# A stored order for the instructions of four engines in a fused attention and MLP kernel

## The chip, the cores and the metric

The kernel runs on one core of one Trainium2 chip. The metric is device microseconds of one execution, the median of 3 runs. Five engines work in the core, each through its own queue, in order: TensorE (PE in the profile, its weight loads PEld), VectorE (DVE), ScalarE (ACT), GpSimd (POOL) and SyncE (SP, which only issues DMAs).

## The reference

Attention with 4 sink positions and a window of 128, then a two-layer MLP over all tokens, all in float32:

```python
batch, n_heads, seq, head_dim = (4, 8, 768, 64)
scores = scale * np.matmul(q, k.transpose(0, 1, 3, 2))
keep = is_sink | in_window            # pos < 4, or 0 <= i - j < 128
a = softmax(np.where(keep, scores, -1e9))
attn_out = np.matmul(a, v)
x = attn_out.transpose(0, 2, 1, 3).reshape(3072, 512)
h = x @ w_in                          # 512 x 2048
out = (h - np.tanh(h)) @ w_out        # 2048 x 512
```

## The kernel before

The 3072 tokens are cut into 12 chunks `cc` of 256 tokens. Attention of a chunk is done in 4 units `u` (a unit is a pair of heads, 48 in all), the MLP of a chunk in 8 groups `g` of 256 hidden columns, 96 steps `n` in all. The chunks' MLP steps run on PE almost without a break from about 50 us on, and the attention of later chunks is slipped in between.

The pieces of a unit, with the lines that a row shows: `scores` multiplies queries and keys on PE (L537 for the first 12 units, L544 after), `merge` masks and takes the row maximum on DVE (L559, L561), `exponent` is ACT's exponential (L569), `sums` the reciprocal on DVE (L589, L590), `scale` on ACT (L595), `sinks` on POOL (L604 to L606). `turn` then transposes the probabilities on PE into the PSUM bank `t` (L629), and three pieces copy them out of that bank into the tile `pt`: in a chunk that starts a batch `whole` on ACT (L636), and always two masked products on DVE, `below` and `after` (both L643). When 2 or 4 units are done, `attend` transposes the sink columns on PE (L670), copies them on ACT into `zr` (L677), multiplies with the values on PE (L686, L692; that reads `zr` and `pt`), and splits the result into a high and a low part on ACT (L709) and DVE (L713).

An MLP step multiplies x by a group of w_in on PE (`h`, L828), takes tanh on ACT (L859), the difference on DVE (L862), and splits it into high and low halves (L865 and L868, in the later chunks L873 to L881 for seven combined blocks); PE then multiplies these by w_out (L910, or L944 in the later chunks). The weights come as 64-bit floats: three DVE instructions decode a group's words (L157, L159, L161), ACT rounds (L752) and DVE forms the low part (L756). Later chunks read w_in's parts back from DRAM into a ring of 7 tiles, and w_out's combined blocks are formed on SP, POOL, ACT and DVE (`derive`, L1048 to L1061).

None of this is issued where it is written. Every piece is handed to `Work.add` with its engine, a duration, a due time and the names that it reads and writes, 3002 pieces in all; `Work.order` decides how they follow each other, and a loop at the end of `_banded` emits them in that order. In this version `order` is a list scheduler: it keeps a clock for each engine, and whenever an engine is free it takes, of the pieces whose inputs are done by its clocks, the one with the earliest due time. The durations, due times and waking delays are constants in the code. The order fixes the queue of each engine, and where pieces of two engines touch the same tile, which of them waits for the other.

Of the kernel before, what the change touches and what calls it, by code (L numbers as in the profile page):

```python
# [17 lines left out]
B, H, S, D = 4, 8, 768, 64  # L18
P = 128
DM = H * D  # L20
# [20 lines left out]
def kernel(  # L41
# [50 lines left out]
    with tc.If(bad == 0) as cmp:  # L92
        _banded(tc, qd, kp, vp, vs, small, masks, w_in, w_out, ident, pts, early, out)
# [76 lines left out]
class Work:  # L170

    WAKE = {"PE": 250, "ACT": 170, "DVE": 90, "POOL": 100, "SP": 80}

    def __init__(self, slack, pad, late, land):
        self.all, self.wrote, self.read = [], {}, {}
        self.slack, self.pad, self.late, self.land = slack, pad, late, land  # L180

    def add(self, engine, took, due, fn, reads=(), writes=(), lands=0, port=False):
        n = len(self.all)
# [9 lines left out]
        self.all.append((engine, took, due, fn, after - {n}, lands, port))  # L193

    def order(self):
        todo = {}
        for n, (engine, *_) in enumerate(self.all):
            todo.setdefault(engine, []).append(n)
        users, left = [[] for _ in self.all], [len(t[4]) for t in self.all]
        for n, t in enumerate(self.all):  # L200
            for a in t[4]:
                users[a].append(n)
        ready = {n: 0.0 for n, k in enumerate(left) if k == 0}
        waiting = {e: [n for n in v if n in ready] for e, v in todo.items()}
        free, port, start, done = dict.fromkeys(todo, 0.0), {}, {}, {}

        def at(n, e):
            t = max(free[e], ready[n])
            return max(t, port.get("DVE" if e == "POOL" else "POOL", 0.0)) if self.all[n][6] else t

        while any(waiting.values()):
            t, e = min((min(at(n, e) for n in v), e) for e, v in waiting.items() if v)
            n = min((n for n in waiting[e] if at(n, e) <= t), key=lambda n: (self.all[n][2], n))
            _, took, _, _, _, lands, locks = self.all[n]
            took *= self.pad if e in ("ACT", "DVE", "POOL") and self.all[n][2] > self.late else 1.0
            waiting[e].remove(n)
            start[n], free[e], done[n] = t, t + took, t + took
            if lands:
                free[e], done[n] = t + (took if e == "POOL" else lands), t + lands + (1700 if self.all[n][2] < self.late else self.land)
            if locks:  # L220
                port[e] = t + took
            for u in users[n]:
                f = self.all[u][0]
                lag = 0 if f == e else self.WAKE[e]
                if f == "PE":
                    lag += self.slack if self.all[u][2] > self.late else 100
                ready[u] = max(ready.get(u, 0.0), done[n] + lag)
                left[u] -= 1
                if not left[u]:
                    waiting[f].append(u)  # L230
        return sorted(start, key=lambda n: (start[n], n)), start


def _banded(tc, qd, kp, vp, vs, small, masks, w_in, w_out, ident, pts, early, out):
    nc = tc.nc
    et = mybir.EngineType
    with ExitStack() as ctx:
# [28 lines left out]
        RAW, TWO, CUT, DUO, SC, PB, ZL, TK = 12, 12, 2, 3, 4, 4, -4000, 1100  # L266
        SLK, PAD, LATE, LAND, QP, KP, BP, LEAD3 = 0.0, 1.05, 68932.8, 4939.1, 0, 0, 0, 92253.7
        SA, NSLOT, RING, GP, LQ, ST = 5, 7, 7, 0, 1, 1
        work = Work(SLK, PAD, LATE, LAND)

        chunks = [(b, 0) for b in range(3)] + [(b, c) for b in range(3) for c in range(1, CPB)]
        chunks += [(b, c) for b in range(3, B) for c in range(CPB)]
# [2 lines left out]
        order += [(cc, g) for g in range(CUT, NG) for cc in (2, 1)] + [(0, g) for g in range(CUT, NG)]  # L275
        order += [(cc, g) for cc in range(3, NCHUNK) for g in range(NG)]
        NS = len(order)
        FIRST, EARLY, PACE, LEAD = 45488.2, 4498.8, 8248.4, 74582.8
        UNIT, SECOND, WLEAD, WNEXT = 2182.8, 6399.4, 6045.8, 1426.5
# [6 lines left out]
        def due_unit(u):  # L286
            cc, p = divmod(u, NPAIR)
            if cc < 3:
                return UNIT * u + SECOND * cc
            return due_step(order.index((cc, 0))) - (LEAD3 if cc == 3 else LEAD) - 2 * PACE * (NPAIR - 1 - p)  # L290

        def due_group(g):
            return due_step(min(n for n, x in enumerate(order) if x[1] == g))
# [23 lines left out]
        def slot(u):  # L317

            return u % PB if u < RAW else u % 2

        def unit(u):
            cc, p = divmod(u, NPAIR)
            return (cc, p, *chunks[cc])
# [116 lines left out]
        mask, above, below, after, rest = masks  # L440
# [45 lines left out]
        qh, ql, ks, pr, st, xps, xh, xl, sps, tps = ({} for _ in range(10))  # L486
# [130 lines left out]
        def place(u):  # L617
            return u % 2 if u < DUO * NPAIR else u % NPAIR

        def turn(u):  # L620

            cc, p, b, c = unit(u)
            m = place(u)

            def transposes():
                to = tps[u] = tbank.rearrange("p (h t q) -> p h t q", h=2, t=2)
                for t in range(2):
                    for h in range(2):
                        nc.tensor.transpose(to[:, h, t, :], pr[u][:, 2 * h + t, NSK:], ident)  # L629

            w = pts[:, m].rearrange("p h (t o) q -> p (h t) o q", o=2)
            w1 = pts[:, m].rearrange("p h (t o) q -> p h t o q", o=2)

            def whole():

                nc.scalar.copy(w1[:, :, 0, 1, :], tps[u][:, :, 0, :])  # L636

            def part(o, mask):
                if c == 0:
                    src, dst, n = tps[u][:, :, 1, :], w1[:, :, 1, o, :], 2  # L640
                else:
                    src, dst, n = tps[u].rearrange("p h t q -> p (h t) q"), w[:, :, o, :], 4
                nc.vector.tensor_tensor(dst, src, mask.unsqueeze(1).to_broadcast([P, n, P]), op=ALU.mult)  # L643

            def plain():
                nc.scalar.copy(w[:, :, 0, :], tps[u].rearrange("p h t q -> p (h t) q"))

            def masked():
                nc.gpsimd.tensor_tensor(w[:, :, 0, :], w[:, :, 0, :], after.unsqueeze(1).to_broadcast([P, 4, P]), op=ALU.mult)

            d = due_unit(u) + 5500
            work.add("PE", 470, d, transposes, [("p", slot(u), 0), ("p", slot(u), 1)], ["t"])
            if c == 0:
                work.add("ACT", 260, d + 1400, whole, ["t"], [("pt whole", m)])
            work.add("DVE", 430 if c == 0 else 710, d + 1500, lambda: part(1, below), ["t"], [("pt own", m)])
            if c and BP:
                work.add("ACT", 490, d + 1500, plain, ["t"], [("pt before", m)])
                work.add("POOL", 1360, d + 1600, masked, (), [("pt before", m)], port=True)
            else:
                work.add("DVE", 430 if c == 0 else 710, d + 1500, lambda: part(0, after), ["t"], [("pt before", m)])  # L660

        def attend(cc, p0, pairs):

# [477 lines left out]
        def attention(cc):  # L1141
            if cc and chunks[cc][0] != chunks[cc - 1][0]:
                sink_values(chunks[cc][0], due_unit(NPAIR * cc) + 4000)
            for u in range(NPAIR * cc, NPAIR * cc + NPAIR):
                if not raw(u):
                    split(u)
                for t in range(2):
                    scores(u, t)
                if u == 0:
                    work.add("DVE", 400, 3000, sink_half, ["sidei", ("p", 0, 1)], ["half"])  # L1150
                    sink_values(0, 10000)
                if RAW <= u + 1 < NU:
                    load_qk(u + 1)
                normalise(u)
                turn(u)
                if cc < DUO and u % 2:
                    attend(cc, u % NPAIR - 1, 2)
            if cc >= DUO:
                attend(cc, 0, NPAIR)
            if cc + 1 < NCHUNK:  # L1160
                load_v(cc + 1)
# [11 lines left out]
        for n in range(NS):  # L1173
            cc, g = order[n]
# [5 lines left out]
            if n:  # L1180
# [3 lines left out]
                cc, g = order[n - 1]  # L1184
# [9 lines left out]
                            derive(i, m)  # L1194
        second_half(NS - 1)

        todo, _ = work.order()
        with tc.manual_schedule(engines={et.PE, et.SP, et.DVE, et.Activation, et.Pool}):
            for n in todo:
                work.all[n][3]()  # L1200
# [204 lines left out]
```

## Time and profile before

| what | value |
|---|---|
| median of 3 runs | 667.82 us (667.61 to 668.23) |
| the profiled execution's own time | 667.38 us |
| its span, first to last instruction | 665.6 us |
| PE, PEld busy | 648.9 us (97%), 603.5 us (91%) |
| DVE, ACT, POOL busy | 543.4 us (82%), 397.0 us (60%), 165.2 us (25%) |
| TensorE's mean granted clock | 0.997 of 2.4 GHz |
| DMA | 152.97 MB, mean 230 GB/s |
| last PE instruction starts | 658.21 us |

A row of the timeline gives the start and the length of an instruction, or of several equal ones that follow each other (x6). PE's instructions overlap, and the ends of its rows are modelled: a 128x256 matmul has a row of 0.28 us, while the next starts some 0.11 us after it. What PE loses is therefore read from the starts, or from the idle time named in brackets with what ended it. DVE's and ACT's rows overlap by a little too.

### The profile page before, as it was taken

Reading aid. Unit: us, or ns where it says so; the run is one execution under the profiler, and the core shown is the slowest. Engines: PE = TensorE matmul, PEld = TensorE weight load, DVE = VectorE, ACT = ScalarE, POOL = GpSimd, SP = SyncE. Lnnn points to the kernel's source line nnn. Section 1 sums busy time; section 2 is a strip of 40 time slices with the busy share of each in tenths; the row PEclk is TensorE's granted clock in tenths of the full one; section 3 lists DMA queues with packets and bytes.
Section 4 is the critical chain, followed back from the end, with each engine's and each line's share of the span. In section 5 each row is a group of like instructions: output and inputs, shape, how many; then the busy total and the mean of one; then the engine's idle time right before and its main releaser. Section 6 shows DMA issues by size and latency. Waiting matters only on the chain.

```text
span 665.6 us, 14571 instructions
## 1 busy us (share of the span) xinstructions
PE 648.9 (97%) x5111; PEld 603.5 (91%) x5111; DVE 543.4 (82%) x1399; ACT 397.0 (60%) x1024; POOL 165.2 (25%) x331
## 2 busy tenths in 40 slices
PE   7889999999999999999999999999999999999995
PEld 6668999999979889899999999999999999999995
DVE  5889999964999778578799899887899899855654
ACT  5987444345898667567665575676666566523331
POOL 5453000000873232243331212312213212100100
PEclk9999999999999999999999999999999999999998
DMA  5877788884999767899977767867776866656861
GB/s 167 290 260 283 249 277 301 289 305 128 231 204 282 219 207 227 241 265 300 301 221 221 231 199 233 252 188 212 246 222 203 263 187 204 209 166 202 262 209 37
DMA packets 79502, 152.97 MB, mean 230 GB/s; under 512 B 9596, under 2 KB 25852, under 8 KB 79420
## 3 DMA queue, kind: packets, MB, share of 16 engines
q1 hardware_dynamic: 65900, 121.52, 57.9%
q0 software_dynamic: 13376, 30.30, 16.4%
q8 instruction: 42, 0.69, 0.4%
q14 instruction: 40, 0.33, 0.1%
q10 hardware_dynamic: 144, 0.13, 0.1%
HBM read 131.47 MB, written 20.45 MB: 228 GB/s over the span
## 4 chain that ended last, share of the span: by engine, by line
PE 82%; DVE 8%; ACT 4%; issue 1%; POOL 1%; DVEq 0%; ACTq 0%; POOLq 0%
PE h L828 36%; PE s L944 11%; PE o L910 8%; PE o L944 8%; PE x L692 3%; PE s L910 3%; PE t L629 2%; PE t L692 2%; PE t L544 2%; PE x L544 2%; PE t L910 2%; PE x L910 2%; DVE pt L643 1%; PE s L544 1%; ACT p L595 1%
## 5 line engine op out<-in xcount | busy, mean ns | idle before, releaser
L828 PE MATMUL h<-xall,ring 128*128 128x256 f32 x990 | 130.1, 279 | 0.0
L828 PEld LDWEIGHTS h<-xall,ring 128*128 128x128 f32 x990 | 121.0, 188 | 1.4 <-issue 0.5
L859 ACT ACTIVATE gbuf<-h 128x512 f32<-128x512 f32 x96 | 57.2, 596 | 90.4 <-PE h L828 68.3
L828 PE MATMUL h<-xall,spare 128*128 128x256 f32 x738 | 97.4, 278 | 0.0
L878 ACT CAST ghbuf<-gbuf 128x896 fp32r<-128x896 f32 x55 | 51.7, 941 | 68.2 <-DVE gbuf L875 67.9
L828 PEld LDWEIGHTS h<-xall,spare 128*128 128x128 f32 x738 | 90.6, 188 | 0.5
L370 POOL DMA_DIRECT2D qraw<-qd x36 | 26.7, 742 | 255.4 <-DVE q L511 199.9
L881 DVE TENSOR_TENSOR glbuf<-gbuf,ghbuf 128x896 fp32r<-128x896 f32 x55 | 59.9, 1089 | 20.2 <-ACT ghbuf L878 17.3
L569 ACT ACTIVATE p<-p,st 128x132 f32<-128x132 f32 x132 | 52.4, 399 | 13.1 <-DVE st L561 12.1
L862 DVE TENSOR_TENSOR gbuf<-h,gbuf 128x512 f32<-128x512 f32 x55 | 37.9, 689 | 22.1 <-ACT gbuf L859 20.9
L910 PE MATMUL o<-w,ghbuf 128*128 128x512 f32 x192 | 49.9, 395 | 0.2 <-ACT ghbuf L865 0.2
L828 PEld LDWEIGHTS h<-xall,w 128*128 128x128 f32 x384 | 46.9, 188 | 2.1 <-DVE w L756 0.4
L828 PE MATMUL h<-xall,w 128*128 128x256 f32 x384 | 48.2, 279 | 0.2 <-DVE w L756 0.2
L502 DVE TENSOR_TENSOR ks<-kraw,ks 64x392 fp32r<-64x392 f32 x72 | 40.4, 562 | 6.0 <-ACT ks L497 3.9
L595 ACT ACTIVATE p<-p,st 128x132 f32<-128x132 f32 x132 | 42.6, 395 | 4.1 <-DVE st L590 3.5
L910 PEld LDWEIGHTS o<-w,ghbuf 128*128 128x128 f32 x192 | 33.8, 188 | 6.1 <-ACT ghbuf L865 0.5
L862 DVE TENSOR_TENSOR h<-h,gbuf 128x512 f32<-128x512 f32 x41 | 28.5, 695 | 13.1 <-ACT gbuf L859 12.8
L497 ACT CAST ks<-kraw 64x392 fp32r<-64x392 f32 x72 | 37.1, 515 | 2.2 <-DMA kraw<-kp 1.3
L865 ACT CAST ghbuf<-h 128x512 fp32r<-128x512 f32 x41 | 24.0, 586 | 21.1 <-DVE h L862 20.4
L944 PE MATMUL s<-edge,ghbuf 128*128 128x256 f32 x220 | 35.1, 278 | 0.0
L944 PE MATMUL o<-w,ghbuf 128*128 128x256 f32 x220 | 35.0, 278 | 0.0
L944 PE MATMUL s<-w,ghbuf 128*128 128x256 f32 x220 | 35.0, 277 | 0.0
(187 smaller groups left out, 1546.7 us busy)
## 6 DMA issues: line engine op xcount, KB each, us to landing
ring<-wscr SPq DMA_DIRECT2D x165, 256.0 KB, 4.8
spare<-wscr SPq DMA_DIRECT2D x123, 256.0 KB, 4.7
qraw<-qd POOLq DMA_DIRECT2D x36, 256.0 KB, 5.2
wraw<-w_in SPq DMA_DIRECT2D x16, 512.0 KB, 5.7
wraw<-w_out SPq DMA_DIRECT2D x16, 512.0 KB, 5.7
wscr<-w SPq DMA_DIRECT2D x16, 512.0 KB, 7.6
kraw<-kp POOLq DMA_DIRECT2D x36, 196.0 KB, 4.6
v<-vp POOLq DMA_DIRECT2D x18, 256.0 KB, 4.2
```

Of the source, the lines that this page charges most:

```text
L497: nc.scalar.copy(ks[u][r, h, :], kt[u][r, :])
L502: (nc.gpsimd if KP else nc.vector).tensor_tensor(k[o, h, :], t[r, :], k[r, h, :].bitcast(F32), op=ALU.subtract)
L544: nc.tensor.matmul(ps[h][:, :WIN], lhsT=q[:, h, t * P : (t + 1) * P], rhs=rhs, start=i == 0, stop=i == 1,)
L569: nc.scalar.activation(e, e, AF.Exp, bias=st[u][:, j : j + 1], scale=-1.0, accum_out=st[u][:, 4 + j : 5 + j],)
L595: nc.scalar.activation(pr[u][:, j, :], pr[u][:, j, :], AF.Copy, scale=s[:, 8 + j : 9 + j])
L828: nc.tensor.matmul(hps[n][:, f, :], lhsT=w, rhs=x, start=r == 0, stop=r == 11)
L859: nc.scalar.activation(g0, h(), AF.Tanh)
L862: nc.vector.tensor_tensor(g0 if strassen(n) else h(), h(), g0, op=ALU.subtract)
L878: nc.scalar.copy(ghbuf[:, n % 2], gbuf[:, 1:, :])
L881: nc.vector.tensor_tensor(low7(n), gbuf[:, 1:, :], ghbuf[:, n % 2].bitcast(F32), op=ALU.subtract)
L910: nc.tensor.matmul(sums_of(n, cc, t), lhsT=a[:, f, t * P : (t + 1) * P], rhs=wt[1, g][:, (0, 1, 0)[i], f, :], start=first and not low and ...
L944: nc.tensor.matmul(acc, lhsT=a[:, b, :], rhs=factor(g, m, part % 2), start=g == 0 and part == 0 and m in (4, 1, 2, 7), stop=closes(n) and ...
```

## The change

The list scheduler is taken out. `Work.order` unpacks a string of 2-byte numbers, which is the finished order of the 3002 pieces, and asserts that it holds every piece once and that no piece stands ahead of one whose result it needs. The constants of the schedule stay in `_banded`, but nothing reads them for the order any more. In `turn`, the three pieces that fill `pt` now also name the tile of decoded weights that lies in the same memory, so that the recorded dependences hold them apart; this also orders a unit's pieces after one another for half of the units from the 13th on.

```diff
-    def __init__(self, slack, pad, late, land):
+    ORDER = (
+        "c-jrugBlpd5<ubIncbb8+1R#i+qP}nwr$(C(Z;r&Hfdv{4V!yk;(Y(n3e;Go)C6UfS3#kQq>PHH#;N&gyo#YFsw675nxqz~c*>~-"
...
+    )
+
+    def __init__(self):
         self.all, self.wrote, self.read = [], {}, {}
-        self.slack, self.pad, self.late, self.land = slack, pad, late, land
...
     def order(self):
-        todo = {}
...
-        return sorted(start, key=lambda n: (start[n], n)), start
+        from base64 import b85decode
+        from struct import iter_unpack
+        from zlib import decompress
+
+        todo = [n for n, in iter_unpack("<H", decompress(b85decode(self.ORDER)))]
+        at = {n: i for i, n in enumerate(todo)}
+        assert len(at) == len(todo) == len(self.all)
+        assert all(at[a] < at[n] for n in todo for a in self.all[n][4])
+        return todo
...
             if c == 0:
-                work.add("ACT", 260, d + 1400, whole, ["t"], [("pt whole", m)])
-            work.add("DVE", 430 if c == 0 else 710, d + 1500, lambda: part(1, below), ["t"], [("pt own", m)])
+                work.add("ACT", 260, d + 1400, whole, ["t"], [("pt whole", m)] + [("dw", m - 2)] * (m > 1))
+            free = [("dw", m - 2)] * (m > 1)
+            work.add("DVE", 430 if c == 0 else 710, d + 1500, lambda: part(1, below), ["t"], [("pt own", m)] + free)
...
-                work.add("DVE", 430 if c == 0 else 710, d + 1500, lambda: part(0, after), ["t"], [("pt before", m)])
+                work.add("DVE", 430 if c == 0 else 710, d + 1500, lambda: part(0, after), ["t"], [("pt before", m)] + free)
```

No instruction is added or taken away; all 3002 pieces stand in both. Compared piece by piece, 563 of DVE's 748 stand at another place of their queue, 457 of ACT's 593, 187 of SP's 429 and 141 of POOL's 194, most of them by one to four places. The first piece that moves is the 8th of DVE's and of ACT's queue, the 10th of SP's and the 13th of POOL's. PE's 1038 pieces keep their order up to the 684th, at 462 us of the profiled execution; of the rest 112 stand elsewhere, by at most 8 places. The lines from `order` on are 35 or 36 higher in the new file.

Three places follow. The first is ACT's queue around the copy of the sink columns into `zr` for the second half of chunk 1 (at 43.29 us of the profiled execution). Before:

```order
L636 COPY pt<-t 128x2x128
L709 CAST xall<-x 128x512
L636 COPY pt<-t 128x2x128
L569 ACTIVATE p_672,st<-p_672,st 128x132 x2
L677 ACTIVATE zr<-x,nswi 128x256 x2
L595 ACTIVATE p_614<-p_614,st 128x132 x4
```

and now:

```order
L671 COPY pt<-t 128x2x128
L745 CAST xall<-x 128x512
L604 ACTIVATE p_625,st<-p_625,st 128x132 x2
L604 ACTIVATE p_668,st<-p_668,st 128x132 x2
L713 ACTIVATE zr<-x,nswi 128x256 x2
L671 COPY pt<-t 128x2x128
L630 ACTIVATE p_625<-p_625,st 128x132 x4
```

The copy out of bank `t` (`whole` of unit 7) stood two pieces ahead of `zr` and now stands behind it; an exponential of unit 8 took its place.

The second is DVE's queue at the same time, the two masked products of unit 7. Before:

```order
L643 TENSOR_TENSOR pt<-t,below 128x2x128
L643 TENSOR_TENSOR pt<-t,after 128x2x128
L589 TENSOR_SCALAR st<-st 128x4
L590 RECIPROCAL st<-st 128x4
L559 COPY_PREDICATED o_252<-above,o_252 128x128
L561 ISA p_672,st<-o_252,mask 128x132
L561 ISA st 128x1
L559 COPY_PREDICATED o_253<-above,o_253 128x128
L561 ISA p_672,st<-o_253,mask 128x132
L561 ISA st 128x1
```

and now:

```order
L624 TENSOR_SCALAR st<-st 128x4
L625 RECIPROCAL st<-st 128x4
L678 TENSOR_TENSOR pt<-t,below 128x2x128
L594 COPY_PREDICATED o_252<-above,o_252 128x128
L596 ISA p_668,st<-o_252,mask 128x132
L596 ISA st 128x1
L594 COPY_PREDICATED o_253<-above,o_253 128x128
L596 ISA p_668,st<-o_253,mask 128x132
L596 ISA st 128x1
L678 TENSOR_TENSOR pt<-t,after 128x2x128
```

The second masked product went behind the reciprocal and behind the whole merge of unit 9.

The third is DVE's queue around the low part of w_in's second group (`w_1` from `wraw_1`), at 64 to 70 us. Before:

```order
L713 TENSOR_TENSOR xl_885<-x,xh_884 128x512
L161 SCALAR_TENSOR_TENSOR pt<-wraw_1_620,pt 128x1024
L475 SCALAR_TENSOR_TENSOR vsink<-vsink,nswi,vraw 64x128 x2
L756 TENSOR_TENSOR w_1_939<-pt,w_1_939 128x8x128
L756 TENSOR_TENSOR w_1_985<-pt,w_1_985 128x1024
```

and now:

```order
L749 TENSOR_TENSOR xl_878<-x,xh_877 128x512
L159 SCALAR_TENSOR_TENSOR pt<-wraw_1_623,pt 128x1024
L792 TENSOR_TENSOR w_1_942<-pt,w_1_942 128x8x128
L161 SCALAR_TENSOR_TENSOR pt<-wraw_1_623,pt 128x1024
L898 TENSOR_TENSOR h_913<-h_913,gbuf 128x512
```

The low part moved ahead of the last decoding instruction of the next weights and of the two instructions for the sink values, which went some ten pieces further back.

## Rows read from the trace of the kernel before

**Rows 1.** The page, part 1: busy time, share of the span, instructions.

```profile
PE 648.9 (97%) x5111; PEld 603.5 (91%) x5111; DVE 543.4 (82%) x1399; ACT 397.0 (60%) x1024; POOL 165.2 (25%) x331
```

**Rows 2.** Three stretches: busy us (instructions) of PE, PEld, DVE, ACT, POOL; PEclk, DMA, GB/s.

```profile
16.60:33.30 16.70, 14.39 (x93) 10.62 (x92) 14.86 (x63) 15.96 (x62) 7.41 (x20) 1.00 0.88 290
33.30:50.00 16.70, 14.48 (x94) 10.65 (x93) 14.88 (x59) 14.54 (x54) 8.92 (x19) 1.00 0.77 259
...
100.00:150.00 50.00, 50.00 (x330) 45.49 (x330) 41.54 (x48) 21.48 (x33) 1.35 (x2) 1.00 0.84 298
```

**Rows 3.** PE's waits over the whole span: total us, times, longest us.

```profile
...
PE x L686 <- ACT zr L677: 1.7, 2, 0.9
PE s L537 <- POOL z L605: 1.5, 1, 1.5
PE t L629 <- ACT pt L636: 0.9, 2, 0.6
PE o L537 <- DVE nswi L561: 0.6, 1, 0.6
PE x L670 <- DVE xall L713: 0.5, 1, 0.5
...
PE h L828 <- DVE w L756: 0.2, 1, 0.2
PE o L910 <- ACT ghbuf L865: 0.2, 1, 0.2
PE t L544 <- DVE pt L643: 0.2, 1, 0.2
```

**Rows 4.** Timeline of PE, 440.5 to 442 us (start, length, engine, line, operation).

```profile
440.27 0.28 PE L944 MATMUL s<-w,ghbuf 128*128 128x256 f32 x1
440.38 0.62 PE L944 MATMUL o<-w,ghbuf 128*128 128x256 f32 x4
...
441.54 0.51 PE L544 MATMUL t<-ks,q 128*128 128x260 f32 x2 [0.20 <-DVE pt L643]
```

**Rows 5.** Timeline of PE, 41.9 to 44.4 us.

```profile
44.17 0.50 PE L686 MATMUL x<-zr,vsink 128*128 128x512 f32 x1 [0.92 <-ACT zr L677]
```

**Rows 6.** Timeline of ACT, 39.1 to 45.3 us.

```profile
42.23 0.37 ACT L636 COPY pt<-t 128x256 f32<-128x256 f32 x1 [1.84 <-PE t L629]
...
43.29 0.83 ACT L677 ACTIVATE zr<-x,nswi 128x256 fp32r<-128x256 f32 x2
```

**Rows 7.** Timeline of DVE, 40.4 to 45 us.

```profile
42.64 0.42 DVE L643 TENSOR_TENSOR pt<-t,below 128x256 f32<-128x256 f32 x1 [0.98 <-ACT pt L636]
42.98 0.41 DVE L643 TENSOR_TENSOR pt<-t,after 128x256 f32<-128x256 f32 x1
43.31 0.16 DVE L589 TENSOR_SCALAR st<-st 128x4 f32<-128x4 f32 x1
...
44.67 0.29 DVE L561 CUSTOM_DVE_ANT_0 wide<-s,mask 128x132 f32<-128x132 f32 x1
```

**Rows 8.** Timeline of DVE, 64 to 70.5 us.

```profile
66.12 1.41 DVE L161 SCALAR_TENSOR_TENSOR pt<-wraw,pt 128x1024 uint32<-128x1024 uint32 x1
67.81 0.71 DVE L475 SCALAR_TENSOR_TENSOR vsink<-vsink,nswi,vraw 64x128 fp32r<-64x128 f32 x2 [0.27 <-POOL vraw L471]
68.53 2.36 DVE L756 TENSOR_TENSOR w<-pt,w 128x1024 fp32r<-128x1024 f32 x2
```

**Rows 9.** Timeline of PE, 191 to 194 us.

```profile
191.69 0.44 PE L670 MATMUL x<-ident,z 128*128 128x128 f32 x2
...
193.43 0.50 PE L686 MATMUL x<-zr,vsink 128*128 128x512 f32 x1 [0.75 <-ACT zr L677]
```

**Rows 10.** Timeline of ACT, 188.6 to 194.9 us.

```profile
192.56 0.82 ACT L677 ACTIVATE zr<-x,nswi 128x256 fp32r<-128x256 f32 x2
```

**Rows 11.** Timeline of ACT, 350.5 to 358.5 us.

```profile
352.24 0.40 ACT L569 ACTIVATE p<-p,st 128x132 f32<-128x132 f32 x1
...
354.70 0.59 ACT L859 ACTIVATE gbuf<-h 128x512 f32<-128x512 f32 x1
```

More of the change, by code (lines that the diff above doesn't have):

```diff
@@ L195, in order @@
     def order(self):
-        todo = {}
[L197 to L230, printed above, removed]
-        return sorted(start, key=lambda n: (start[n], n)), start
+        from base64 import b85decode
[6 more added lines that the diff above has]
+        return todo
 def _banded(tc, qd, kp, vp, vs, small, masks, w_in, w_out, ident, pts, early, out):
@@ L268, in _banded @@
         SA, NSLOT, RING, GP, LQ, ST = 5, 7, 7, 0, 1, 1
-        work = Work(SLK, PAD, LATE, LAND)
+        work = Work()
         chunks = [(b, 0) for b in range(3)] + [(b, c) for b in range(3) for c in range(1, CPB)]
@@ L1195, in _banded @@
         second_half(NS - 1)
-        todo, _ = work.order()
+        todo = work.order()
         with tc.manual_schedule(engines={et.PE, et.SP, et.DVE, et.Activation, et.Pool}):
```

64 lines of the change are left out of this document (63 added, 1 removed).

## The prediction

> **What bounds the kernel now.** I read the page's busy times first. PE is busy for 97% of the span and DVE for 82% [rows 1]. PE's share says little by itself, since the row of a matmul is longer than the step to the next: the first matmul of [rows 4] has a row of 0.28 us, and the next starts 0.11 us after it. What matters is whether PE ever stands still, and for that the table by stretch: from 100 to 150 us it is busy for all of 50.00 us, while from 16.6 to 50 us it is idle for some 2.3 us in each 16.7, with DVE busy for 14.9 and ACT for 14.5 to 16.0 [rows 2]. In that early stretch DVE and ACT set the pace; later PE does. TensorE's granted clock is 1.00 in all of them, so no wait there costs clock.
>
> The list of PE's waits then gives the whole ceiling of this change [rows 3]. The 1.5 us before a score of unit 4 lie in the first 19 us, and the loads of unit 4 keep their places on SP; what PE waits ahead of its first matmuls precedes everything that is ordered. The other waits listed come to 1.7 + 0.9 + 0.6 + 0.5 + 0.2 + 0.2 + 0.2 = 4.3 us in 9 places. A wait is counted from the modelled end of the row before it, which is 0.28 - 0.11 = 0.17 us too late [rows 4], so I add 0.17 us to each: **5.8 us is what an order that never lets PE wait could bring**, 0.9% of the time.
>
> The Trainium skill says otherwise (Perfetto Trace Analysis, section Identifying the Most-Contended Engine): judge TensorE's headroom by the busy share of weight loads, not of matmuls. By that rule the headroom would be 665.6 - 603.5 = 62.1 us, ten times mine, and an order without waits would end at 605.7. The stretch from 100 to 150 us contradicts it: weight loads are busy for 45.49 of 50 us there, and no wait is listed.
>
> **The change, wait by wait.** No instruction comes or goes, so the sum is made of waits that end earlier and waits that appear.
>
> (a) The longest wait, 0.92 us before the values of chunk 1 [rows 5], ends with ACT's copy into `zr`, which runs from 43.29 to 44.12 [rows 6]. ACT now does `whole` of unit 7 (0.37) behind it, so `zr` can be done by 43.8. But the same matmuls need unit 7's second masked product, which ended at 43.39 [rows 7] and now stands behind a reciprocal and a merge, 44.67 - 43.31 = 1.36 us of DVE's work: 44.75, half a us too late. DVE, however, idled for 0.98 us ahead of the first product, waiting for ACT's `whole` [rows 7], and now it need not, since `whole` comes after that product. 44.75 - 0.98 = 43.8, the same as the ACT side. I take **0.4 us** gained. The ends are -0.6 (DVE cannot use its idle time) and 1.1 (the wait goes altogether).
>
> (b) The other early waits, for `pt` (0.9), a merge (0.6) and a low part (0.5), are 2.0 us, with the 0.17 in each of four places 2.7 [rows 3]. The pieces that end them are moved both ways, and DVE has little idle time to work with [rows 2]. I take **0.3 us**; the ends are -0.6, as in (a), and 2.7.
>
> (c) PE waits 0.2 + 0.17 = 0.4 us for the low part of w_in's second group [rows 3]. That part starts at 68.53, behind a decoding instruction of 1.41 us and the sink values' 0.71 [rows 8]. Both now stand behind it, so it is done some 2 us earlier and the wait is gone: **0.4 us**. What is late instead is w_out's second group, which is not wanted before the step's second half. Ends: 0 and 0.4.
>
> (d) Before the values of chunk 3 PE waits 0.75 + 0.17 = 0.9 us for `zr` [rows 9]. Its input is there at 191.69 + 0.44 = 192.13, but ACT does an exponential first and copies from 192.56 to 193.38 [rows 10]. In the new order `zr` stands ahead of that exponential and can run at 192.13: **0.4 us**; the rest stays. Ends: 0 and 0.9.
>
> (e) The wait of w_out's product for ACT's high part, 0.2 + 0.17 [rows 3]. ACT does that cast two key casts earlier now; the copy out of the same PSUM bank comes after them instead. I take **0.2 us**; ends 0 and 0.4.
>
> (f) The score that waits 0.20 us for a masked product at 441.5 [rows 4]: that product now precedes ACT's copy out of bank `t` instead of waiting for it, but the bank is free only after both. **0.2 us**; ends 0 and 0.4.
>
> Gains: 0.4 + 0.3 + 0.4 + 0.4 + 0.2 + 0.2 = 1.9 us.
>
> (g) In seven units an exponential went behind a tanh that it used to precede. In the one of [rows 11] it ran at 352.24 and would now follow the tanh that ends at 354.70 + 0.59 = 355.29, so 3.0 us later. Queued behind it on ACT are the unit's second exponential and its scaling; for the scaling PE's transpose waits. That is a loss where the unit's slack is below 3 us. I take **-0.4 us** for all seven; the ends are 0 and -2.8, a whole wait of 0.4 as in (c) for each.
>
> (h) SP's and POOL's DMAs moved too, weight loads and the later keys, queries and values. No wait in [rows 3] after 20 us ends with a DMA, so I cost it at nothing; what hides them is the lead that they have over PE. Where that lead is gone, each late load is a wait like (a), 0.9. PE's own moves after 462 us I also cost at nothing: its pieces are the same, and only (f)'s kind of wait, 0.2, is listed anywhere near. I keep -0.9 and 0.4 as ends for (h).
>
> Sum: 1.9 - 0.4 = 1.5 us. The profiled execution took 667.38 us, its span 665.6, and the start and the end around it do not change: 665.9 for that execution. The median of the runs shown lies 0.44 higher, so the forecast is 667.82 - 1.5 = **666.3 us**.
>
> **The rivals.**
>
> *Every wait goes.* The order was searched as a whole, and the waits of [rows 3] are each ended by one piece that could come earlier; against it, DVE's load in the first 50 us, which no order lowers [rows 2]. 667.8 - 5.8 = 662.0 us.
>
> *Given back.* What PE gains at one place it waits for at the next: in (a) the new limit is DVE in place of ACT, and (b) is mostly of that kind. With (c) to (f) at their low ends, (a) and (b) at nothing and (g) at nothing, the time stays at 667.8 us. For it speaks that later stretches have no idle time on PE to win [rows 2].
>
> *Masked products too late.* This is the one on the other side. 31 of DVE's 96 masked products now stand behind a merge or an MLP piece that they stood ahead of. The price is that of (a) without its idle time: 1.36 us of work more ahead of the product, less the 44.17 - 43.39 = 0.78 us that it had to spare, so 0.6 us each. Four of them eat up the 1.9 us of gains; from six on the kernel is slower by over 0.2%, and eight give 667.8 - 1.9 + 8 x 0.6 = 670.7 us. With six to eight I put it at 670 us. Against it: all but five lie after 50 us, where PE has MLP steps to do while DVE catches up.
>
> That the order is not the stated one is no rival for most of the span, since PE's queue is the same up to 462 us; after that it isn't.
>
> **How the numbers follow.** A measurement of this kernel can tell some 0.2%, 1.3 us, from no change: 666.5 and 669.1 are the bounds. The forecast gets 0.38; its own range is 665.0 to 667.5, 0.24 of it below 666.5 and 0.14 above. Every wait gone: 0.16, all faster. Given back: 0.27, of which 0.06 faster, 0.17 same, 0.04 slower. Late products: 0.19, of which 0.03 same and 0.16 slower. Together 0.46 faster, 0.34 same, 0.20 slower. The range leaves out about half of the first rival below and of the last above: 662.3 to 669.9.
>
> **What would show it.** If (a) holds, the wait for `zr` near 44 us is gone or is named after DVE's second product, and the values start near 43.8. If (c) holds, the first matmul of step 3 follows with no gap near 69 us. If (d) holds, the wait near 193 us is 0.3 to 0.5. If (g) is worse, transposes wait for ACT's scaling in units 11, 30, 31, 35, 39, 45 and 46. The last rival shows as PE waits that end with DVE's L678. I am wrong if the sum of PE's listed waits after 20 us falls by more than 4 us or rises, or if a DMA ends any of them.

## The result and the profile after

The changed kernel takes **673.5 us** (median of 4 runs, 672.79 to 673.99) beside 667.87 for the kernel before in the same session: a ratio of 1.0086, 95% interval 1.0073 to 1.0100. By the ratio it is 5.7 us slower; 1.5 us faster was forecast, and the range ended at 669.9. The profiled execution has a span of 671.8 us beside 665.6, the clock is 0.997 in both, and the busy times hardly move: DVE 545.4 us beside 543.4, ACT 396.2 beside 397.0.

TensorE's waits in the changed kernel, from 20 to 215 us and from 215 us on (waited for, total, times, longest):

```profile
PE x L706 <- POOL z L641: 1.3, 1, 1.3
PE x L722 <- ACT zr L713: 0.4, 1, 0.4
PE t L664 <- DVE pt L678: 0.2, 1, 0.2
PE t L664 <- ACT pt L671: 0.2, 1, 0.2
...
PE t L664 <- ACT p L630: 1.6, 4, 0.8
PE x L706 <- POOL z L641: 0.7, 1, 0.7
PE t L579 <- DVE pt L678: 0.2, 1, 0.2
```

This is the list of [rows 3] for the changed kernel, and it nearly hides the loss: the waits after 20 us come to 4.6 us beside 4.3 before. What TensorE loses has to be read from starts. I took the same piece of TensorE's queue in both traces and subtracted its starts; the queue is the same up to 462 us, and the last matmul is the same.

| changed kernel, us | TensorE against the kernel before, us |
|---|---|
| 27.1 | +0.20 |
| 76.2 | -2.32 |
| 214.6 | -2.43 |
| 258.7 | +0.31 |
| 361.1 | +2.08 |
| 408.4 | +3.71 |
| 464.6 | +4.42 |
| 664.4, last matmul | +6.21 |

So there are two stories: a gain of 2.4 us in the first 215 us, and a loss of 8.6 us between 215 and 573 us, 8.4 of it by 560. After that nothing changes. The stretches of the loss, of the kernel before and then of the changed one (length, PE, PEld, DVE, ACT, POOL busy, each with its instructions, clock, DMA share, GB/s):

```profile
220.00:260.00 40.00, 40.00 (x297) 35.95 (x297) 30.68 (x93) 27.09 (x78) 11.85 (x27) 1.00 0.68 205
360.00:460.00 100.00, 99.65 (x891) 97.06 (x891) 89.61 (x241) 63.58 (x165) 22.56 (x48) 1.00 0.71 219
460.00:560.00 100.00, 100.00 (x888) 97.62 (x887) 89.31 (x239) 61.11 (x155) 22.88 (x47) 1.00 0.72 222
```

```profile
220.00:260.00 40.00, 38.70 (x277) 33.56 (x277) 31.50 (x93) 27.02 (x80) 14.82 (x32) 1.00 0.82 239
360.00:460.00 100.00, 99.04 (x870) 95.16 (x870) 87.09 (x231) 61.43 (x157) 25.57 (x54) 1.00 0.75 226
460.00:560.00 100.00, 99.58 (x876) 96.02 (x874) 89.16 (x236) 63.38 (x159) 17.04 (x40) 1.00 0.67 209
```

TensorE's matmul rows overlap, so its busy time barely falls; the matmuls that get done do (891 to 870). From 360 to 460 us DVE does 2.5 us less work in 100 us: it is not busier, it stands still more (in the two other stretches it does 0.8 us more and 0.15 less).

The largest wait shows how. The next three fences are ACT, TensorE and GpSimd of the changed kernel around unit 19 (start, length, instruction, and in brackets the idle time before it and what ended it):

```profile
223.86 0.41 ACT L604 ACTIVATE p<-p,nswi 128x132 f32<-128x132 f32 x1
224.17 0.19 ACT L604 ACTIVATION_READ_ACCUMULATOR p<-p,nswi 128x1 f32 x1
225.96 0.62 ACT L543 CAST q<-qraw 128x512 fp32r<-128x512 f32 x1 [1.60 <-DMA qraw<-qd]
226.49 1.29 ACT L630 ACTIVATE p<-p,nswi 128x132 f32<-128x132 f32 x4
```

```profile
225.07 1.09 PE L946 MATMUL o<-w,ghbuf 128*128 128x512 f32 x4
226.94 0.33 PE L664 MATMUL t<-ident,p 128*128 128x128 f32 x1 [0.77 <-ACT p L630]
227.53 0.62 PE L664 MATMUL t<-ident,p 128*128 128x128 f32 x3 [0.26 <-ACT p L630]
```

```profile
215.83 0.56 POOL L396 DMA_DIRECT2D kraw<-kp  x1 [6.32 <-DVE ks L537]
217.97 0.72 POOL L405 DMA_DIRECT2D qraw<-qd  x1 [1.58 <-ACT ghbuf L901]
```

Unit 20's queries are now issued behind its keys, at 217.97 us, and are there at 225.96. ACT's cast of them stands ahead of unit 19's scaling, so ACT idles for 1.60 us, the scaling comes late, and TensorE waits at the transposes: 0.94 us more than before in the step ahead of them and 0.62 in them.

The other waits need no late load. Unit 32 in the kernel before, DVE, ACT and then TensorE:

```profile
386.49 1.08 DVE L881 TENSOR_TENSOR glbuf<-gbuf,ghbuf 128x896 fp32r<-128x896 f32 x1
387.50 0.16 DVE L589 TENSOR_SCALAR st<-st 128x4 f32<-128x4 f32 x1
387.69 0.18 DVE L590 RECIPROCAL st<-st 128x4 f32<-128x4 f32 x1
387.90 1.15 DVE L502 TENSOR_TENSOR ks<-kraw,ks 64x392 fp32r<-64x392 f32 x2
```

```profile
387.97 0.60 ACT L859 ACTIVATE gbuf<-h 128x512 f32<-128x512 f32 x1
388.59 1.30 ACT L595 ACTIVATE p<-p,st 128x132 f32<-128x132 f32 x4
```

```profile
389.67 0.61 PE L629 MATMUL t<-ident,p 128*128 128x128 f32 x4
```

and in the changed kernel:

```profile
389.16 0.56 DVE L537 TENSOR_TENSOR ks<-kraw,ks 64x392 fp32r<-64x392 f32 x1
389.75 0.69 DVE L546 TENSOR_TENSOR q<-qraw,q 128x512 fp32r<-128x512 f32 x1
390.36 1.08 DVE L917 TENSOR_TENSOR glbuf<-gbuf,ghbuf 128x896 fp32r<-128x896 f32 x1
391.36 0.16 DVE L624 TENSOR_SCALAR st<-st 128x4 f32<-128x4 f32 x1
391.56 0.18 DVE L625 RECIPROCAL st<-st 128x4 f32<-128x4 f32 x1
```

```profile
391.54 0.60 ACT L895 ACTIVATE gbuf<-h 128x512 f32<-128x512 f32 x1 [0.45 <-DVE st L624]
392.17 1.29 ACT L630 ACTIVATE p<-p,st 128x132 f32<-128x132 f32 x4
```

```profile
392.81 1.03 PE L664 MATMUL t<-ident,p 128*128 128x128 f32 x4
```

One key split of 0.56 us went from behind the reciprocal to ahead of it, and ahead of the gate's low part (L917) too. ACT's scaling (L630) stands behind a tanh that had not waited before and now idles 0.45 us for DVE; it ends at 393.46, after TensorE's turn has come at 392.81. The four transposes take 1.03 us instead of 0.61: 0.4 us of waiting, which the wait list does not show as a row of its own. There was no room for it. Over the 28 units whose transposes run between 215 and 560 us, the end of ACT's scaling lies 0.32 us ahead of TensorE's first transpose in the kernel before (median; past it in 5 units), and 0.15 us behind it in the changed one (past it in 17).

The transposes are the largest part of the loss and not the whole. Up to 465 us, where TensorE's queue is the same, it loses 6.9 us by the starts: 2.9 ahead of and in these transposes, 1.4 ahead of and in scores, 1.4 in products with w_out, 0.9 at the transposes of sink columns and the rest in many small steps.

### The profile page after: what moved, and what is told of

Read it like the earlier page. It is cut to its first block, busy times and chain, and to the rows that moved or that the text cites. A ratio compares the mean times of both kernels' runs of the same rounds, so it can differ in the third digit from the quotient of the medians.

```text
span 671.8 us, 14547 instructions
## 1 busy us (share of the span) xinstructions
PE 654.1 (97%) x5111; PEld 604.6 (90%) x5111; DVE 545.4 (81%) x1399; ACT 396.2 (59%) x1024; POOL 154.6 (23%) x331
## 4 chain that ended last, share of the span: by engine, by line
PE 79%; DVE 10%; ACT 5%; DMA 2%; issue 2%; POOL 1%; DVEq 0%; ACTq 0%; POOLq 0%
PE h L864 33%; PE s L980 9%; PE o L946 8%; PE o L980 6%; PE x L728 4%; PE s L946 3%; PE t L664 3%; PE t L728 2%; DMA qraw<-qd 2%; PE t L946 2%; PE x L946 2%; PE s L579 2%; PE t L579 2%; PE x L579 1%; ACT p L630 1%
## 5 line engine op out<-in xcount | busy, mean ns | idle before, releaser
L895 ACT ACTIVATE gbuf<-h 128x512 f32<-128x512 f32 x96 | 57.1, 595 | 94.9 <-PE h L864 70.5
L917 DVE TENSOR_TENSOR glbuf<-gbuf,ghbuf 128x896 fp32r<-128x896 f32 x55 | 59.8, 1088 | 14.2 <-ACT ghbuf L914 12.9
L396 POOL DMA_DIRECT2D kraw<-kp x36 | 20.7, 574 | 141.6 <-DVE ks L537 111.0
L630 ACT ACTIVATE p<-p,st 128x132 f32<-128x132 f32 x132 | 42.6, 394 | 5.4 <-DVE st L625 5.1
L898 DVE TENSOR_TENSOR h<-h,gbuf 128x512 f32<-128x512 f32 x41 | 28.4, 693 | 10.5 <-ACT gbuf L895 10.3
```

Source lines behind the costliest of these rows:

```text
L630: nc.scalar.activation(pr[u][:, j, :], pr[u][:, j, :], AF.Copy, scale=s[:, 8 + j : 9 + j])
L895: nc.scalar.activation(g0, h(), AF.Tanh)
L898: nc.vector.tensor_tensor(g0 if strassen(n) else h(), h(), g0, op=ALU.subtract)
L917: nc.vector.tensor_tensor(low7(n), gbuf[:, 1:, :], ghbuf[:, n % 2].bitcast(F32), op=ALU.subtract)
```

## The experiments

All but two keep every piece, and the new lines of `turn`, and change only the stored numbers. "List order" is what the old scheduler finds for the changed program. Below, TensorE's shifts are counted from 20 us on, since the first 20 us alone differ by up to 1 us from one trace to another.

**The list order on the changed program (listed), and the stored order cut at 214.5 us.**

```diff
-todo = stored
+todo = listed
```

> The stored order is replaced by the one that the old list scheduler finds for the changed program, with the three new dependences of turn. TensorE's queue is then exactly that of the changed kernel, also after 462 us, and SyncE's is exactly that of the kernel before; DVE, ACT and POOL differ from the kernel before in 91, 65 and 8 places, all late. Theory Q (the loss comes from the order of the pieces on DVE and ACT from 220 us on): 667.9 us, within 0.8 of the kernel before. Theory L (it comes from loads that SyncE and GpSimd now issue later): also 667.9. Theory P (it comes from TensorE's new order after 462 us and the new dependences): over 670, with the 1.8 us of loss after 462 us at least.

Measured: 0.9999 (0.9990 to 1.0008), the same as the kernel before. Theory P is out: neither the new dependences nor TensorE's own new order after 462 us costs anything that can be measured.

```diff
-todo = stored
+todo = stored[:k] + [n for n in listed if n not in stored[:k]]
```

> The stored order up to the TensorE piece at 214.5 us (968 of MLP step 25), the list order of the kernel 'listed' behind it. In the changed kernel TensorE was 2.4 us ahead of the kernel before at that piece. Theories Q and L: the gain stays, 667.9 - 2.4 = 665.4 us (664.9 to 666.0). Rival G (given back: whatever TensorE gains early it waits for later, since DVE and ACT come no earlier): 667.5 to 668. Theory P: 669 or more.

Measured: 683.39 us, 1.0218 (1.0204 to 1.0232), and all expectations missed. Two waits stand at the cut:

```profile
PE s L579 <- ACT q L543: 11.2, 1, 11.2
PE s L579 <- DVE ks L537: 3.5, 1, 3.5
```

There the two orders had issued different pieces of w_out's blocks, and GpSimd's queue was torn, joined from parts that did not fit. It says nothing of the theories.

```diff
-todo = stored
+todo = listed[:k] + [n for n in stored if n not in listed[:k]]
```

> The reverse: the list order up to the same TensorE piece, the stored order behind it. Theories Q and L: the early gain is missing and the loss of 8.6 us is all there, 667.9 + 8.6 = 676.5 us (675.5 to 677.5). Rival G (the waits after 220 us are there because TensorE arrives 2.4 us early): 673 to 674, no slower than the changed kernel. Theory P: some 669.7, since only the loss after 462 us is there.

Measured: 674.36 us, 1.0090 (1.0075 to 1.0105). Without the early gain the kernel is no slower than with it. The time is rival G's, but its reason holds only for the first waits: in the trace unit 19 waits 0.19 us and unit 21 0.10 (1.56 and 0.58 in the changed kernel), while the waits from 280 us on are all there, seven of the nine largest within 0.05 us of their length (units 32 and 42 differ by 0.2 and 0.3).

**SyncE and GpSimd in list order (compute).**

```diff
-queue["SP"], queue["POOL"] = stored
+queue["SP"], queue["POOL"] = listed
```

> The stored order on TensorE, DVE and ACT throughout, but behind the TensorE piece at 214.5 us SyncE and GpSimd follow the list order (10 of their pieces a place or two aside, where the two orders exclude each other). Theory Q: the loss is nearly all there, 672.5 to 674 us. Theory L: the loss goes and the early gain stays, 665.4 to 667. Half and half would be 669.5.

Measured: 711.45 us, 1.0623 (1.0596 to 1.0650). The halves of two orders exclude each other at many places (a wait of 10.3 us for ACT, one of 8.4 for the weight ring), so the time decides nothing.

**A cut where both orders have issued the same pieces (early153, late153).** The edits are those of `early` and `late` with another k.

> The stored order up to TensorE's piece of step 17 at 153 us, the list order behind it. This place is chosen since the two orders have there issued the same pieces but one (a store of weights on SyncE), so no queue is torn; in the run 'early' the junction itself cost 17.8 us. In the changed kernel TensorE was 2.2 us ahead at this piece. If the early gain is kept when the list order follows: 667.9 - 2.2 = 665.7 us, a ratio of 0.9967 (0.9955 to 0.9980). Rival G (given back further on, whatever order follows): 667.5 to 668, a ratio of 0.9995 to 1.0005.

Measured: 665.79 us, **0.9960 (0.9945 to 0.9976)**: by its time the early gain is real and is kept, and this kernel beats both. In its trace TensorE's lead falls from 2.3 us at 153 us to 1.3 at the end; in that of `listed` TensorE falls back by 1.3 us over the same stretch.

> The reverse: the list order up to the same piece, the stored order behind it. If gain and loss add up: 673.5 + 2.2 = 675.7 us, a ratio of 1.012. Rival G: the waits of 2.3 us at units 19 and 21 are shorter when TensorE comes 2.2 us later, as in the run 'late': 673.5 to 674.3, a ratio of 1.0085 to 1.010.

Measured: 675.25 us, 1.0097 (1.0082 to 1.0112), as rival G has it. So the stored order behind 153 us costs 6.5 us by itself (0.0097 x 668), the one ahead of it brings 2.7, and together they cost 5.7, not 3.8: some 1.9 us of the early gain are given back, an amount that the three intervals leave uncertain by some 1.7. The traces show it at unit 19: behind 153 us TensorE loses 7.0 us here and 8.4 in the changed kernel, and unit 19 waits 0.19 us here and 1.56 there; unit 21's 0.6 us stay.

**One pair in ACT's queue exchanged (swap19).**

```diff
-L543 CAST q<-qraw 128x512
 L630 ACTIVATE p<-p,nswi 128x132 x4
+L543 CAST q<-qraw 128x512
```

> The changed kernel with one pair exchanged in ACT's queue: the scaling of unit 19 ahead of the cast of unit 20's queries instead of behind it. In the changed kernel the cast waits until 225.96 us for its load, the scaling, whose input is there at 224.77, ends at 227.77, and TensorE stands still for some 1.5 us before and within the transposes of unit 19. Theory Q': the scaling runs at 224.8 to 226.1, the wait falls under 0.2 us and the gain stays to the end: 672.1 us (1.4 faster than the changed kernel, a ratio of 1.0065). Rival G: the wait goes here and comes back at the next units, 673.2 to 673.6 (1.0082 to 1.0088).

Measured: 672.2 us, 1.0050 (1.0038 to 1.0062). ACT and then TensorE in its trace:

```profile
224.26 1.30 ACT L630 ACTIVATE p<-p,nswi 128x132 f32<-128x132 f32 x4 [0.51 <-DVE nswi L625]
225.47 0.60 ACT L543 CAST q<-qraw 128x512 fp32r<-128x512 f32 x1
```

```profile
225.39 0.60 PE L664 MATMUL t<-ident,p 128*128 128x128 f32 x4
```

The wait is gone. Of its 1.56 us TensorE keeps 0.9 at 260 us and 0.5 at the end; the ratio says 2.4, with the first 20 us in it. By the time theory Q' holds; the trace bears it out only in part.

**The softmax pieces of the nine waiting units put back on DVE and ACT (chains).** One of the 23 moves:

```diff
+L624 TENSOR_SCALAR st<-st 128x4
+L625 RECIPROCAL st<-st 128x4
 L537 TENSOR_TENSOR ks<-kraw,ks 64x392
 L546 TENSOR_TENSOR q<-qraw,q 128x512
 L917 TENSOR_TENSOR glbuf<-gbuf,ghbuf 128x896
-L624 TENSOR_SCALAR st<-st 128x4
-L625 RECIPROCAL st<-st 128x4
```

> The changed kernel with the merges, sums, exponentials and scalings of nine units (19, 21, 31 to 34, 41, 42, 44) put back ahead of the pieces of the next unit and of the MLP that they precede in the kernel before, on DVE (12 moves) and ACT (11, and the exchange of 'swap19'); SyncE's, GpSimd's and TensorE's queues are as stored. The waits of TensorE at these nine units were 5.2 us in the changed kernel. Theory Q: most of it comes back, 669.5 us (668.5 to 670.5, a ratio of 1.0010 to 1.0040). Rival L (late loads): only unit 19's 1.4 us comes back, 672. Rival G (given back elsewhere): 673 or more.

Measured: 672.62 us, 1.0058 (1.0045 to 1.0070). Theory Q fails in its simple form. The time is the one of rival L, but more goes than the wait of the late load: of the waits named, 0.58 us go at unit 21, 0.81 at 31, 0.32 at 33, 0.37 at 42 and 0.45 at 44, while those at 32, 34 and 41 mostly stay. TensorE is 3.3 us ahead of the changed kernel at 380 us, and has given back 2.7 of it by the end. The first place where it does, TensorE and then ACT:

```profile
384.82 2.09 PE L864 MATMUL h<-xall,spare 128*128 128x256 f32 x17
387.80 0.72 PE L980 MATMUL s<-edge,ghbuf 128*128 128x256 f32 x4 [0.89 <-ACT ghbuf L914]
```

```profile
385.48 0.41 ACT L604 ACTIVATE p<-p,st 128x132 f32<-128x132 f32 x1
385.79 0.19 ACT L604 ACTIVATION_READ_ACCUMULATOR p<-p,st 128x1 f32 x1
385.88 0.51 ACT L532 CAST ks<-kraw 64x392 fp32r<-64x392 f32 x1
386.29 0.62 ACT L543 CAST q<-qraw 128x512 fp32r<-128x512 f32 x1
386.81 0.94 ACT L914 CAST ghbuf<-gbuf 128x896 fp32r<-128x896 f32 x1
```

Unit 32's exponentials now precede the gate's high part of step 50, and the MLP step waits for that instead.

**The cut at 367 us, and the halves behind it (early366, compute366, dma366).**

> The stored order up to TensorE's score of unit 31 at 367 us, the list order behind it; the two orders have issued the same pieces there but one. In the changed kernel TensorE is 2.2 us behind the kernel before at this piece and 6.2 at the end. If the loss behind 367 us is the stored order's own: 667.9 + 2.2 = 670.1 us, a ratio of 1.0033 (1.0020 to 1.0048). If it is only what was left over from the stretch before (DVE and ACT once late stay late): 1.006 or more. This kernel is also what the next two are compared with.

Measured: 670.28 us, 1.0030 (1.0020 to 1.0041), as expected: the transposes' waits of units 32, 33, 34, 42 and 44 are gone once the list order follows. Just behind the cut, up to 380 us, TensorE still loses 1.8 us in its trace, and 0.3 after that. The three kernels that follow the stored order to 153 us, to 367 us and to the end stand at 0.9960, 1.0030 and 1.0086: the loss builds up all along.

> As 'early366', but behind the cut DVE and ACT keep the stored order and only SyncE and GpSimd follow the list (4 of GpSimd's pieces a place or two aside). Theory Q (the loss is in the queues of DVE and ACT): 4.0 us more than 'early366', a ratio of 1.0080 to 1.0098. Theory L (late loads): like 'early366', 1.0025 to 1.0045.

> The other half: behind the cut SyncE and GpSimd keep the stored order, ACT follows the list and DVE too, but for 22 places where the two exclude each other. Theory Q: like 'early366', a ratio of 1.0025 to 1.0050. Theory L: 1.0080 to 1.0098. If each half alone is harmless and only both together cost, this one and 'compute366' are both under 1.005.

Measured: 680.84 us, 1.0188 (1.0173 to 1.0203), and 678.84 us, 1.0159 (1.0139 to 1.0180): each half costs more than the whole, so the times do not decide between Q and L. In the traces 4.7 and 3.0 us of it lie from 440 to 460 us, where one wait is of a torn queue (3.0 us for a masked product on DVE in `dma366`). What `compute366` does show, with SyncE and GpSimd in list order, are the waits at units 32, 33 and 44 with the lengths of the changed kernel (0.41, 0.32, 0.45 beside 0.43, 0.32, 0.45), and in `dma366`, with DVE and ACT in list order, these three are gone: they belong to the queues of DVE and ACT. Units 34 and 42 wait in both halves.

**TensorE's transposes one MLP piece later (pelate).**

```diff
-L664 MATMUL t<-ident,p 128*128 128x128 x4
 L864 MATMUL h<-xall,ring 128*128 128x256
+L664 MATMUL t<-ident,p 128*128 128x128 x4
```

> The changed kernel with one thing moved in TensorE's queue: from unit 18 on the transposes of 28 units stand one MLP piece later (0.23 to 0.91 us of matmuls); the other four queues are as stored. Theory J: TensorE's queue was made by the list, which puts a unit's transposes where its own DVE and ACT have just finished (0.36 us ahead of them in the middle, in the trace of before); the stored order of DVE and ACT ends the same work 0.45 us later against TensorE (0.09 us behind its turn in the middle), so every unit waits a little. Then the later place takes these waits, 3.4 us at the transposes themselves and part of 0.9 beside unit 19: 670.0 us (669.3 to 671.0, a ratio of 1.0020 to 1.0045). If the wait only moves on to the masked products, the next scores or the values: 673 or more (1.0080).

Measured: 677.69 us, 1.0134 (1.0118 to 1.0149), slower still. The waits for ACT's scaling go, and these come, after 215 us:

```profile
PE t L579 <- DVE pt L678: 2.1, 4, 1.1
PE t L579 <- ACT ghbuf L914: 0.6, 1, 0.6
```

The transposes later are the masked products later, DVE stands still until they come, and the next unit's scores wait for DVE. A unit is a loop between TensorE and DVE, and room made at this one place of it was lost at the next.

**Less work for DVE (light_stored, light_listed).** Both leave out the 55 subtractions named in the expectation.

```diff
-nc.vector.tensor_tensor(g0 if strassen(n) else h(), h(), g0, op=ALU.subtract)
+if not strassen(n):
+    nc.vector.tensor_tensor(h(), h(), g0, op=ALU.subtract)
```

> The changed kernel without the 55 subtractions of the seven-block MLP steps (from 316 us on; the gate is then tanh(h) in place of h - tanh(h)): 37.8 us less work on DVE, some 11 us in each 100, and no piece of the softmax is touched. In the changed kernel TensorE loses 5.3 us against the kernel before from 300 us on. Theory D: those waits are there since DVE, 90% busy, has too little room to make up for the places where the stored order lets it stand at the head of its queue; with a tenth less to do they vanish: 668.5 us (667.5 to 669.5, a ratio of 1.000 to 1.0025). Rival S: each wait is the length of a single chain of pieces from one TensorE piece to the next, and the load does not matter: 672 or more (1.006).

> The same subtractions left out of the kernel 'listed'. TensorE hardly waits there, so both theories: 667 to 668, a ratio of 0.998 to 1.0005. 'light_stored' less 'light_listed' is what the stored order costs with a less loaded DVE: under 1.5 us by theory D, over 4 by rival S.

Measured: 1.0015 (1.0002 to 1.0027) and 0.9993 (0.9984 to 1.0003), a difference of 0.0022 or 1.5 us, beside 5.8 between the changed kernel (1.0086) and `listed` (0.9999). By the times most of the loss comes from DVE's load. The traces show far less: between these two TensorE loses 3.2 us from 300 us on, and between `listed` and the changed kernel 4.0 (the 5.3 of the expectation are counted against the kernel before). The waits at units 33 and 34 are as long as in the changed kernel, and from unit 28 on the scalings still end 0.19 us behind the transposes' turn, in the middle. The subtraction also stands between a step's tanh and its high part, so leaving it out shortens that chain as well as the load. That DVE's load has a part in the loss is shown by the times alone, and how large it is stays open.

**The weight pieces put back (derive).**

```diff
-queue[e] = stored[e]
+queue[e] = stored[e] with the 128 pieces of derive where listed[e] has them
```

> The changed kernel with the 128 pieces that form w_out's combined blocks (on SyncE, GpSimd, ACT and DVE) put back behind the pieces that they follow in the list order; all others keep the stored order among themselves. In the stored order DVE's last 14 of these come 20 to 74 us later than in the kernel before, in a stretch from 220 to 290 us where TensorE loses 2.7 us. Theory W: that work is what makes DVE and ACT late there: 671.5 us (671 to 672, a ratio of 1.0055). Rival: the waits at units 19 and 21 have to do with a late load and with the order of the pieces of the softmax, and stay: 673 or more (1.0080).

Measured: 695.04 us, 1.0398 (1.0375 to 1.0422): a torn order again, with 7.5 us of waits for a gate's low part that stands behind these pieces on DVE. Theory W stays untried.

## Why the prediction was wrong

Its gains were right, and too small. (a) No idle time is left ahead of the values, which now start at 42.86 us:

```profile
42.86 0.49 PE L722 MATMUL x<-zr,vsink 128*128 128x512 f32 x1
...
191.36 0.50 PE L722 MATMUL x<-zr,vsink 128*128 128x512 f32 x1 [0.44 <-ACT zr L713]
```

The step ahead of it is 0.87 us shorter, where 0.4 was taken. (b) The early waits around units 6 to 10 give 1.15 us, where 0.3 was taken: some grew by up to 0.8, others shrank by as much. (c) 0.51, taken 0.4. (d) 0.31, taken 0.4; the wait that stays is the 0.44 of the row above, as foreseen. (e) 0.40, taken 0.2. (f) 0.26, taken 0.2. Together 3.5 us for 1.9, less 0.3 for a step that grew at unit 15 and some 0.3 in small steps. In all but (b) the wait named is gone or shorter, as foreseen; in (b) waits moved both ways, and that their sum is a gain is luck.

**The step that failed is (g)**, the loss by late pieces, taken at -0.4 us with an end of -2.8, and with it the reading of [rows 3] as all that is at stake. What the runs showed in its place is a loss of 8.6 us by the starts, spread over scalings that come late at units without such an exponential (2.9 us at the transposes up to 465 us, 1.56 of them at unit 19 by (h)), scores and products. I searched the new order for pieces that looked late, found seven exponentials behind a tanh and gave each a part of a wait. Of those seven units 45 and 46 wait less than 0.1 us at their transposes and only 31 has a larger wait, 0.81 us, which is not the one foreseen. GpSimd and DVE of the changed kernel, then TensorE, and last GpSimd of `chains`:

```profile
374.02 1.15 POOL L641 CAST z<-z 128x32 fp32r<-128x32 f32 x1
```

```profile
374.02 1.08 DVE L917 TENSOR_TENSOR glbuf<-gbuf,ghbuf 128x896 fp32r<-128x896 f32 x1
```

```profile
375.22 0.44 PE L706 MATMUL x<-ident,z 128*128 128x128 f32 x2 [0.66 <-POOL z L641]
```

```profile
370.87 0.21 POOL L641 CAST z<-z 128x32 fp32r<-128x32 f32 x1
```

Unit 31's scaling ends at 373.40 and its transposes run without a wait. What TensorE waits for is GpSimd's last cast of the sink columns: it starts together with DVE's low part and takes 1.15 us in place of 0.21. In `chains` it is over before the low part starts, and the wait is gone.

The units whose transposes do wait, 19, 21, 32 to 34, 42 and 44, I had not named. The lead that could be lost I weighed only for the seven exponentials and, in the last rival, for the masked products, and I did not read it from the trace. Before, there is no wait after 215 us but one of 0.2, and I read that as safety; the scalings end 0.32 us ahead of the transposes, so that a single split of 0.56 us set ahead of a reciprocal and a low part is enough. 457 and 563 moved pieces had 28 such places to hit.

(h) was costed at nothing, with -0.9 as an end: one load, unit 20's queries, did become late, and unit 19 lost 1.56 us by it, through ACT's queue, where I had looked for a DMA that ends a wait of TensorE. The trace of the kernel before had a sign of it, where ACT stood still for a load of keys just ahead of unit 19's scaling:

```profile
226.59 0.52 ACT L497 CAST ks<-kraw 64x392 fp32r<-64x392 f32 x1 [1.06 <-DMA kraw<-kp]
```

Of the rivals, *given back* holds for a part of the early gain (some 1.9 of 2.7 us, `late153`), but not for the rest of the loss. *Masked products too late* had the right side and the wrong piece: TensorE waits more for the scaling ahead of the transposes (2.9 us up to 465 us) than for the products behind them (0.5 at the scores that write into bank `t` again). My sign that I am wrong, that the listed waits rise, hardly fired (4.6 beside 4.3 us), although TensorE lost 8.6 us.

The order of the four queues behind 153 us is shown to be what costs the time (`listed`, `early153`). What stays open is how the loss divides between DVE's load and the single chains, and which of the moved pieces behind 280 us start it. Every repair that I tried on one engine or one class of pieces was given back elsewhere or tore the order; only the list order behind 153 us, as a whole, keeps the gain.

## What to carry to other kernels

Where one engine is never idle, a new order of the others has little to win and must be judged by what it can lose: measure how long before its use each input is ready, and treat a median like the 0.3 us here as no slack. Compare two kernels by the starts of the same instruction, since the list of waits leaves out short waits (2.5 us listed after 215 us, 8.6 lost). When a changed order is good in one stretch and bad in another, join the two at a place where both have issued the same pieces.

## What the runs showed of the hardware

Three things I had not expected. The traces repeat: where two kernels have the same order, TensorE's shift between them stays within 0.02 us for a hundred (`late153` against the kernel before: 2.08 us at 60 us, 2.06 at 160), so that a single wait of 0.3 us can be followed from run to run.

GpSimd's last cast of the sink columns into `z` (0.21 us in the middle) can be held for the length of a DVE instruction beside it. The traces of all the runs have 816 of these casts. The 52 that took 0.94 to 1.30 us each had a DVE instruction of 1.08 to 1.23 us beside them, in 44 cases the gate's low part, and ended 0.07 us after it; the other 764 took at most 0.77. So a wait of 0.8 us, as at unit 31, can come from some tenths of a us in the time at which two engines meet.

And the weight loads' busy time follows what TensorE loses where the matmuls' does not. From 220 to 260 us it falls by 35.95 - 33.56 = 2.39 us and the matmuls' by 1.30, while TensorE loses 2.7; from 360 to 560 us by 1.90 + 1.60 = 3.5 us and the matmuls' by 1.0, while TensorE's shift grows by 3.9, from 2.1 to 6.0. Its level is still no headroom: from 220 to 260 us of the kernel before it stands at 35.95 of 40 without a wait. The Trainium skill (Perfetto Trace Analysis, section Identifying the Most-Contended Engine) judges TensorE's headroom by MFU, the share of the peak arithmetic that is done, or by the busy share of the weight loads; the prediction weighed only the second. In these runs that share serves for the difference between two kernels in one stretch, and not for the headroom of one.
